# A new order of steps, k filled up to five chunks of 128 rows, and another order of three products, in linear attention followed by a gated FFN

## The chip, the core and the metric

The kernel runs on one core of one Trainium2 chip. The time is that of the core, in microseconds (us), from runs of the same program; less is better. TensorE is called PE here, VectorE DVE, ScalarE ACT and GpSimd POOL; SyncE (SP) issues the DMAs.

## What is computed

```python
# q, k, v: batch 8, heads 8, sequence 576, head size 64
q_s = exp(q - max(q, -1));      q_s = q_s / (sum(q_s, -1) + 1e-9)
k_s = exp(k - max(k, axis=2));  k_s = k_s / (sum(k_s, axis=2) + 1e-9)      # over the sequence
kv  = einsum('bhsd,bhse->bhde', k_s, v)
x   = einsum('bhsd,bhde->bhse', q_s, kv)          # then 4608 tokens x 512
xn  = x / sqrt(mean(x*x, -1) + 1e-6) * rms_g
out = (silu(xn @ w_gate) * (xn @ w_val)) @ w_out  # 512 -> 1536 -> 512
```

## The kernel before

The 4608 tokens lie in nine blocks of 512 (j = 0 to 8), the 1536 inner features in twelve tiles of 128, the eight heads in four pairs (g = 0 to 3). The batches of the attention (b = 0 to 7) are 576 rows long, so blocks and batches overlap unevenly. The FFN is done in three ways. Block 0 works on the weights as they come, in the steps `f1` (L1230, gate and value) and `f2` (L1301, output). Block 1 uses `f1p` (L1246) on f16 pairs of a high and a low word: 24 products of 512 columns for each of its 12 tiles. Its results leave PSUM by `silu1` (L1252, on ACT) and `h_mul1` (L1257, on DVE), and they leave two buffers, the pool `ps_gv`, for the tiles to come. Blocks 2 to 8 use a scheme of seven products, `pp` (L1166), with evictions `ev` and the output product `fu` (L1214).

The weights arrive packed and are unpacked by chains of small steps on ACT and DVE (`conv_*`, lines 437 to 464), cut in words (`w_hi`, `w_lo`), and made into f16 operands for the later blocks (`w_sc`: L388 on ACT over 1024 columns; `b_hi`, `b_lo`, `t_op`, `t_hi`, `t_lo`: casts at L383, sums at L1118, L1126 to L1144). All that has to be there before `pp` can start.

Of the attention, three steps matter here. `k_mm` (L600) forms k's product with v for one batch and head pair: twenty products, ten for each head, the two heads in the two halves of PSUM's partitions. The sequence of 576 rows is taken in four chunks of 128 and one of 64. `q_x` (L796) multiplies the result with q in three products per segment: kv is held as a high and a low word (`hi`, `lo`), q as `qh` and `ql`. `n_sum` (L920) is the sum of squares for the norm: two products with one constant operand.

What every engine does in which order is written out by hand. `ORDER` is a text of 2970 steps. It is read in one pass, and each step appends its instructions to the queues of the engines; a queue is worked off in that order, and an instruction at its head that has to wait holds up all behind it. A step's name is followed by its numbers and, where more than one engine can do it, by the engine: `:A`, `:D` or `:P` for ACT, DVE or POOL.

```python
    with tc.manual_schedule():
        for step in ORDER.split():
            step, _, engine = step.partition(":")
            name, *args = step.split(".")
            unit[0] = where[engine]
            steps[name](*map(int, args))
```

Two kinds of step only keep PE busy: `warm` at the start, and `fill.n`, which adds n products with zeros (L476) to a sum that is open.

Of the kernel before, what the change touches and what calls it, by code (L numbers as in the profile page):

```python
# [29 lines left out]
q_exp.0.0 v_load.0.2 q_max0.0.2 q_sum0.0.0 load_w.0.1 q_sub0.0.1:P fill.2 k_mm.0.0 q_exp.0.3 k_rec.0.2 q_sum0.0.3  # L30
kv_norm0.0.0:A q_sub0.0.2:P load_w.1.1 q_exp.0.1 g_abs q_eps0.0.0 q_exp.0.2 q_rec0.0.0 q_sum0.0.1 v_load.0.1
q_mul0.0.0:P conv_low.0.0.1 kd_load.1.0 k_max.0.1 conv_mul.0.0 fill.12 q_t0.0.0 q_eps0.0.3 k_exp.0.1 conv_shift.0.0
load_w.3.0 k_tr0.2.0 conv_sign.0.0 q_c0.0.0:A k_tr0.2.1 k_ev0.2.0:A q_rec0.0.3 fill.2 q_x0.0.0 load_w.2.2 q_eps0.0.1
q_rec0.0.1 q_mul0.0.3:P k_ev0.2.1:A q_sum0.0.2 load_w.1.2 q_mul0.0.1:P conv_low.3.2.1 k_tr0.3.0 x_hi.0.0:D x_sq.0.0
load_w.2.1 x_lo.0.0 k_tr0.3.1 k_ev0.3.0:A k_mm.0.2 q_eps0.0.2 k_ev0.3.1:A q_load0.1.0 q_rec0.0.2 conv_low.0.1.1
k_eps.0.1 k_rec.0.1 q_mul0.0.2:P conv_mul.0.1 k_mm.0.3 k_load.1.0 conv_low.1.0.2 k_eps.0.3 k_rec.0.3 conv_shift.0.1
k_tr0.1.0 v_load.1.0 kv_norm0.0.3:A k_tr0.1.1 conv_sign.0.1 n_sum0.0 v_load.1.1 kv_norm0.0.2:A k_max.1.0 w_hi.0.0.2:P
q_t0.0.3 conv_mul.1.0 q_t0.0.1 q_c0.0.3:D load_w.4.1 conv_low.3.0.2 conv_shift.1.0 q_x0.0.3 q_c0.0.1:A conv_sign.1.0
w_lo.0.0:P f1.0.0.0.0 x_sq.0.3 f1.0.1.0.0 x_hi.0.3:D s_tr k_ev0.1.0:A kd_load.1.1 x_lo.0.3 w_lo.0.1:P k_ev0.1.1:A
fill.3 k_mm.0.1 conv_low.2.2.1 s_top load_w.0.2 conv_low.1.2.1 s_rows s_bits kv_norm0.0.1:A load_w.4.0 k_rows.1.0  # L40
conv_low.2.0.2 q_x0.0.1 k_load.1.1 q_max0.1.0 q_t0.0.2 x_sq.0.1 x_hi.0.1:D q_load0.1.1 q_sub0.1.0:P q_c0.0.2:A
n_sum0.1 x_lo.0.1 q_load0.1.2 v_ones.1.0 q_exp.1.0 q_x0.0.2 k_sub.1.0 k_load.1.2 v_ones.1.1 f1.0.1.0.1 q_sum0.1.0
conv_mul.1.1 f1.0.1.0.3 f1.0.0.0.1 load_w.5.0 f1.0.0.0.3 x_hi.0.2:D x_sq.0.2 k_exp.1.0 conv_shift.1.1 fill.1 n_sum0.2
conv_sign.1.1 f1.0.1.0.2 f1.0.0.0.2 conv_low.0.2.1 f1.0.0.1.0 x_lo.0.2 f1.0.1.1.0 w_hi.1.0.2:P load_w.5.1 f1.0.1.1.1
# [5 lines left out]
q_sub0.1.1:P g_mul.0 conv_shift.1.2 f1.2.0 w_lo.2.1:P silu.0 conv_sign.1.2 conv_low.6.0.2 v_ones.1.2 h_mul.0  # L50
load_w.5.2 conv_mul.3.0 q_eps0.1.0 g_mul.1 f1.2.1 conv_shift.3.0 silu.1 conv_sign.3.0 g_mul.2 conv_mul.3.1 load_w.7.0
q_max0.1.2 conv_one.3.1 silu.2 conv_shift.3.1 q_sub0.1.2:P conv_low.5.2.1 q_rec0.1.0 k_rows.1.1 k_eps.1.0 k_rec.1.0
conv_sign.3.1:P h_mul.2 kv_norm0.1.0:A h_mul.1 conv_mul.3.2 w_hi.3.0.2:P load_w.7.1 k_max.1.3 f2.0 conv_shift.3.2
kd_load.2.0 q_exp.1.2 conv_sign.3.2 q_exp.1.1 w_lo.3.0:P k_sub.1.1 load_w.7.2 conv_mul.2.2 q_sum0.1.1 conv_mul.4.0
# [20 lines left out]
w_lo.8.1:P q_exp.1.3 g_mul.7 fill.5 n_col.0.0 k_exp.1.2 n_max.0.0 w_lo.7.1:P f1.7.1 conv_sign.11.2 n_sq.0.2 q_sum0.1.3
v_ones.1.3 h_lo.5:P n_sq.1.0 n_col.0.1 w_hi.9.0.2:A h_lo.6:P k_mm.1.2 n_max.0.1 k_rows.1.3 n_sq.1.1 k_eps.1.2
v_load.2.0 f1.8.0 k_rec.1.2 w_lo.9.1:P k_sub.1.3 k_load.2.1 kv_norm0.1.2:A k_exp.1.3 n_bits.0.1.0 q_eps0.1.3
q_rec0.1.3 w_lo.9.0:P k_mm.1.3 g_mul.8 q_mul0.1.3:P silu.7 q_t0.1.1 k_eps.1.3 k_rec.1.3 f1.8.1 silu.8 q_c0.1.1:D
kv_norm0.1.3:A h_mul.7 n_bits.0.1.1 n_bits.0.1.2 n_bits.0.1.5 w_sc.0.1 n_bits.0.1.3 n_bits.0.1.4 q_x0.1.1 h_mul.8
# [1303 lines left out]
```

## Time and profile before

| | |
|---|---|
| median of 3 runs | 934.89 us (933.1, 934.89, 935.95) |
| span of the profiled execution, first to last instruction | 930.9 us |
| median less this span | 4.0 us |
| PE busy | 913.8 us, 98% of the span |
| DVE busy | 617.3 us, 66% |
| ACT busy | 559.1 us, 60% |
| POOL busy | 305.9 us, 33% |

The span is that of one execution under the profiler. The profile lists no other time for it, so the 4.0 us between it and the median are taken as what lies around the span. A busy share is a mean over stages that differ, and PE's share holds the zero products of `fill` and `warm` too.

### The profile page before, as it was taken

The numbers are of one execution on the slowest core, as the hardware profiler recorded it, in microseconds if no ns is written. First come the engines' busy times: TensorE is split into PE (matmuls) and PEld (weight loads), VectorE is DVE, ScalarE is ACT, GpSimd is POOL, SyncE is SP. The second block draws the span as 40 slices with busy tenths as digits, with TensorE's granted clock in tenths as the row PEclk, the third lists the DMA queues.
The fourth block names the chain that finished last, engine by engine and source line by source line (L and its number), as shares of the span: only waits on it lengthen the run. The fifth ranks groups of instructions, "written<-read, shape, count | busy, mean of one in ns | idle before, by whom it ended". The sixth has DMA issues, their size and how long they took to land.

```text
span 930.9 us, 16383 instructions
## 1 busy us (share of the span) xinstructions
PE 913.8 (98%) x6479; PEld 644.0 (69%) x6479; DVE 617.3 (66%) x1330; ACT 559.1 (60%) x880; POOL 305.9 (33%) x304
## 2 busy tenths in 40 slices
...
DMA packets 29550, 68.06 MB, mean 73 GB/s; under 512 B 3744, under 2 KB 4000, under 8 KB 29472
## 3 DMA queue, kind: packets, MB, share of 16 engines
...
## 4 chain that ended last, share of the span: by engine, by line
PE 83%; DVE 6%; ACT 4%; DMA 3%; issue 2%; POOL 1%; SPq 0%; ACTq 0%; POOLq 0%; DVEq 0%
PE ps_gv L1166 38%; PE ps_o L1214 22%; PE ps_o L1301 5%; PE ps_gv L1230 5%; PE ps_gv L1246 4%; PE ps_a L796 2%; PE ps_a L600 2%; DMA qt<-in_q_dram 1%; PE ps_a L560 1%; DMA w_gv<-in_kt_dram 1%; DMA w_br<-in_w_dram 1%; PE ps_a L1021 1%; ACT w_gv L388 0%; PE ps_a L725 0%; DVE x_raw L827 0%
## 5 line engine op out<-in xcount | busy, mean ns | idle before, releaser
L1166 PEld LDWEIGHTS <-w_gv 128*128 128x128 f16 x2016 | 196.0, 98 | 39.7 <-issue 3.2
L1166 PE MATMUL ps_gv<-xo,w_gv 128*128 128x256 f16 x1296 | 155.8, 273 | 0.6 <-ACT w_br L383 0.4
L1166 PE MATMUL ps_gv<-x_op,w_gv 128*128 128x256 f16 x720 | 86.5, 273 | 0.2
L1166 PEld LDWEIGHTS <-w_br 128*128 128x128 f16 x756 | 73.7, 98 | 14.3 <-issue 1.3
L1214 PEld LDWEIGHTS <-hh 128*128 128x128 f16 x504 | 48.9, 98 | 49.8 <-issue 0.4
L1214 PEld LDWEIGHTS <-hl 128*128 128x128 f16 x504 | 49.0, 98 | 47.5 <-issue 0.6
L1214 PE MATMUL ps_o<-w_o,hl 128*128 128x512 f16 x336 | 79.9, 379 | 0.0
L1214 PE MATMUL ps_o<-w_o,hh 128*128 128x512 f16 x336 | 78.4, 379 | 0.0
L1230 PE MATMUL ps_gv<-xo,wf 128*128 128x512 f32 x264 | 66.7, 404 | 0.0
L1166 PE MATMUL ps_gv<-xo,w_br 128*128 128x256 f16 x540 | 66.1, 273 | 0.0
L1230 PEld LDWEIGHTS ps_gv<-xo,wf 128*128 128x128 f32 x264 | 49.0, 188 | 12.9 <-issue 2.8
L1166 PEld LDWEIGHTS <-wf 128*128 128x128 f16 x504 | 49.2, 98 | 8.1 <-issue 0.3
L1181 DVE TENSOR_TENSOR tm<-ps_gv,tm 128x512 f32<-128x512 f32 x29 | 20.0, 689 | 50.9 <-PE ps_gv L1166 47.7
L785 POOL TENSOR_TENSOR ql<-qT,qh 128x512 fp32r<-128x512 f32 x14 | 18.2, 1301 | 87.1 <-ACT qh L383 87.1
L383 ACT COPY ps_gv<-ps_gv 128x512 f32<-128x512 f32 x42 | 24.0, 572 | 36.3 <-PE ps_gv L1166 13.8
L1181 DVE TENSOR_TENSOR w_br<-ps_gv,w_br 128x512 f32<-128x512 f32 x29 | 20.0, 690 | 37.4 <-PE ps_gv L1166 36.8
L1166 PE MATMUL ps_gv<-xo,wf 128*128 128x256 f16 x360 | 43.9, 273 | 0.0
L897 POOL TENSOR_TENSOR acc<-acc,sq 128x512 f32<-128x512 f32 x11 | 14.0, 1270 | 71.8 <-ACT sq L893 71.8
L1246 PE MATMUL ps_gv<-x_op,w_br 128*128 128x512 f16 x144 | 31.9, 379 | 0.0
L383 ACT COPY w_br<-ps_gv 128x512 f32<-128x512 f32 x29 | 17.0, 585 | 23.5 <-PE ps_gv L1166 23.4
L970 POOL TENSOR_TENSOR wf<-w_gv,wf 128x512 fp32r<-128x512 f32 x22 | 28.1, 1293 | 6.7 <-ACT wf L383 6.3
L383 ACT COPY tm<-ps_gv 128x512 f32<-128x512 f32 x29 | 17.0, 585 | 21.5 <-PE ps_gv L1166 21.3
...
## 6 DMA issues: line engine op xcount, KB each, us to landing
...
```

The costliest lines, as they stand in the source:

```text
L383: (e.copy if e is nc.scalar else e.tensor_copy)(dst, src)
L600: nc.tensor.matmul(ps[h * D:(h + 1) * D, :n1], lhsT=ke[:n, h, j], rhs=vt_[b, g][:n, j, h], start=(j == 0), stop=(j == len(rows) - 1))
L785: on(nc.gpsimd).tensor_tensor(out=ql, in0=qT_[j, g], in1=qh_[j, g][0].bitcast(F32), op=ALU.subtract)
L796: nc.tensor.matmul(px[:, c0:c1], lhsT=wt, rhs=mv[:, c0:c1], start=(i == 0), stop=(i == 2))
L897: on(nc.gpsimd).tensor_tensor(out=acc_[j], in0=acc_[j], in1=sq_[j, g], op=ALU.add)
L970: on(nc.gpsimd).tensor_tensor(out=cut(wl[:, a]), in0=W(s, a), in1=cut(wh[:, a].bitcast(F32)), op=ALU.subtract)
L1166: nc.tensor.matmul(pair(ps, i), lhsT=a[:, wt], rhs=y if i else y.rearrange("p (a c) -> p a c", a=2), start=(first and k == 0 and i == 0 an ...
L1181: nc.vector.tensor_tensor(out=v, in0=bank[j, u, 5 if n == 5 else 3], in1=v, op=ALU.add)
L1214: nc.tensor.matmul(po[2 * n + t], lhsT=a[:, o:o + P], rhs=w, start=(u == 0 and i == 0 and p == 0), stop=(u == NU - 1 and i == 1 and p == 2))
L1230: nc.tensor.matmul(pd[s], lhsT=m[:, a, c * P:(c + 1) * P], rhs=X[j, c][x], start=(n == 1), stop=(n == 3 * NKT))
L1246: nc.tensor.matmul(pd[s], lhsT=w[:, wt], rhs=x, start=(c == 0 and p == 0), stop=(c == NKT - 1 and p == 2))
L1301: nc.tensor.matmul(po[t], lhsT=a[:, t * P:(t + 1) * P], rhs=w, start=(i == 0 and n == 0), stop=(i == NF - 1 and n == len(terms) - 1))
```

## The change

`ORDER` is replaced as a whole (2967 steps instead of 2970); it moves almost all steps and gives some another engine. Only two of its lines stand here, the one with the longest `fill` of before and one of after with a shorter `fill` ahead of a `k_mm`. The steps of PE are the same ones, but for the zero products: 53 before, 32 after. The chunks of `k_mm` are all 128 rows long for the batches 1 to 7; the rows past the end of k are -1e30 in DRAM, so that their exponentials are zero (the DMAs have the same sizes as before, since k came padded to five chunks already, with repeated rows). Batch 0 keeps its chunk of 64. In `q_x` the product (hi, ql) comes second and (lo, qh) third. The keys of `po` are bookkeeping: two blocks may now have output sums open at once.

```diff
@@ ORDER
-o_lo.4:P silu.3 conv_sign.5.2 load_w.10.0 conv_mul.5.1 q_max0.1.3 load_w.10.2 fill.20 q_t0.1.0 conv_one.5.1 w_lo.4.1:P
+conv_low.4.0.2 k_max.1.2 load_w.5.2 fill.4 k_mm.1.0 conv_shift.3.0 kd_load.1.3 w_lo.2.0:P f1.2.0 k_eps.1.0
@@ k_mm
-        rows = [min(P, S - c * P) for c in range(C0)]
+        rows = [P if b else min(P, S - c * P) for c in range(C0)]
@@ q_x
-            for i, (wt, mv) in enumerate(((hi, qh), (lo, qh), (hi, ql))):
+            for i, (wt, mv) in enumerate(((hi, qh), (hi, ql), (lo, qh))):
@@ fu (f2 and store likewise)
-                po[t] = ps_o.tile([P, DM], F32, name="ps_o")
+                po[j, t] = ps_o.tile([P, DM], F32, name="ps_o")
@@ layout
+    past = (np.arange(128)[:, None] + 128 * np.arange(5) >= s)[..., None]
-        "k": pairs(k)[1:, :, :, chunks].transpose(0, 1, 3, 2, 4, 5).reshape(b - 1, g, 128, -1),
+        "k": np.where(past, np.float32(-1e30), pairs(k)[1:, :, :, chunks]).transpose(0, 1, 3, 2, 4, 5).reshape(b - 1, g, 128, -1),
```

After's line numbers are one lower than before's in the parts shown below.

**PE, where block 0 turns from `f1` to `f2`.** L1301 is the output product, L1230 a tile's gate or value, L560 a broadcast of k's maxima, L476 a product with zeros; 20 pairs like the last two rows follow each other, then come four products of L712 (a transpose of q). Before:

```order
L560 MATMUL ps_a<-ident,kx 128x128
L1301 MATMUL ps_o<-w_o,tm 128x512 x4
L1230 MATMUL ps_gv<-xo,wf 128x512 x12
L1301 MATMUL ps_o<-w_o,tm 128x512 x4
L476 LDWEIGHTS zero_b
L476 MATMUL ps_o<-ones_b,zero_b 128x512
```

After, the same stretch of PE's queue, from the first L1301 on:

```order
L1300 MATMUL ps_o<-w_o,tm 128x512 x4
L559 MATMUL ps_a<-ident,kx 128x128
L1229 MATMUL ps_gv<-xo,wf 128x512 x12
L1300 MATMUL ps_o<-w_o,tm 128x512 x4
L1229 MATMUL ps_gv<-xo,wf 128x512 x12
L711 MATMUL ps_a<-ident,x_op_94 128x128 x4
L1300 MATMUL ps_o<-w_o,tm 128x512 x4
L1229 MATMUL ps_gv<-xo,wf 128x512 x12
L469 MATMUL ps_gv<-mean_w 128x512 x2
L1229 MATMUL ps_gv<-xo,wf 128x512 x24
```

The twenty zero products are gone from this place and no others stand in for them, but for the two of a `warm`; the products of the next tiles follow at once.

**ACT, around the first `silu1` (L1252; after: L1251), at the start of block 1.** L388 over 1024 columns scales weights for the later blocks, the casts to `w_br` make their high words. Before:

```order
L383 CAST kv<-ot 128x128
L388 ACTIVATE w_gv<-w_gv,sc 128x1024 x2
L383 CAST w_br<-w_gv 128x512
L388 ACTIVATE w_gv<-w_gv,sc 128x1024
L383 CAST w_br<-w_gv 128x512
L388 ACTIVATE w_gv<-w_gv,sc 128x1024
L383 CAST w_br<-w_gv 128x512
L1252 ACTIVATE tm<-ps_gv,ig 128x512
```

After:

```order
L382 CAST kv<-ot 128x128
L382 CAST hh<-tm 128x512
L1251 ACTIVATE tm<-ps_gv,ig 128x512
L387 ACTIVATE w_gv<-w_gv,sc 128x1024 x4
L1251 ACTIVATE tm<-ps_gv,ig 128x512
```

The scales that stood ahead of the first `silu1` now stand behind it.

**DVE, from the first `h_mul1` (L1257; after: L1256) on.** Between it and the second, before has one small instruction:

```order
L1118 TENSOR_TENSOR w_br<-w_gv,w_br 128x512
L1061 TENSOR_SCALAR mx<-mx 128x6
L1044 TENSOR_SCALAR inv<-mx 128x6
L1257 SCALAR_TENSOR_TENSOR tm<-ps_gv,cu,tm 128x512
L1047 TENSOR_SCALAR ig<-inv 128x6
L1257 SCALAR_TENSOR_TENSOR tm<-ps_gv,cu,tm 128x512
```

After has sixteen, the first eleven of which are shown here behind the first `h_mul1`; a copy of 128x128, three small ones and one more L1117 of 128x512 follow, and then the second `h_mul1`:

```order
L1256 SCALAR_TENSOR_TENSOR tm<-ps_gv,cu,tm 128x512
L1117 TENSOR_TENSOR w_br<-w_gv,w_br 128x512
L382 CAST kv<-ot 128x128
L755 TENSOR_REDUCE sm<-qt 128x16
L1048 TENSOR_SCALAR cu<-sc 128x2
L1284 TENSOR_TENSOR hl<-tm,hh 128x512
L1055 TENSOR_SCALAR mx<-ps_a 128x6
L1057 TENSOR_SCALAR mx<-mx 128x6
L1060 TENSOR_SCALAR mx<-mx 128x6
L1063 SCALAR_TENSOR_TENSOR os<-ig 128x6
L1066 TENSOR_TENSOR mx<-mx,os 128x6
L1129 TENSOR_TENSOR w_gv<-w_gv 128x512
```

From the first `h_mul1` to the twelfth and last, DVE's queue holds 49 instructions of 128x512 before and 60 after, and 12 of 64x64 before and 20 after: steps of `t_op`, `kv_hi`, `x_sum` and `q_sub` have come to it from POOL and ACT. Over the whole program ACT has 723 rows instead of 803, POOL 384 instead of 281, DVE 1098 instead of 1115.

## Rows read from the trace of the kernel before

**Rows 1.** The page, part 1: busy us (share of the span) and instructions.

```profile
PE 913.8 (98%) x6479; PEld 644.0 (69%) x6479; DVE 617.3 (66%) x1330; ACT 559.1 (60%) x880; POOL 305.9 (33%) x304
```

**Rows 2.** The page, part 4: the chain that ended last, by engine.

```profile
PE 83%; DVE 6%; ACT 4%; DMA 3%; issue 2%; POOL 1%; SPq 0%; ACTq 0%; POOLq 0%; DVEq 0%
```

**Rows 3.** Windows: length, busy PE, PEld, DVE, ACT, POOL; PE's clock, DMA share, GB/s.

```profile
0.00:40.00 40.00, 34.39 (x206) 22.63 (x207) 27.95 (x62) 27.98 (x54) 18.66 (x37) 1.00 0.97 366
40.00:80.00 40.00, 38.58 (x168) 25.48 (x167) 35.08 (x72) 33.80 (x52) 24.93 (x24) 1.00 0.71 246
80.00:160.00 80.00, 80.00 (x420) 61.88 (x420) 61.37 (x136) 65.48 (x97) 49.24 (x47) 1.00 0.26 85
160.00:270.00 110.00, 106.24 (x605) 54.05 (x604) 79.85 (x184) 83.53 (x133) 69.83 (x65) 1.00 0.23 75
270.00:800.00 530.00, 527.96 (x4153) 388.69 (x4153) 361.40 (x799) 304.00 (x476) 133.94 (x127) 1.00 0.16 50
800.00:931.00 131.00, 126.67 (x936) 91.25 (x933) 51.62 (x83) 44.34 (x73) 9.25 (x7) 1.00 0.05 17
```

**Rows 4.** PE's timeline over one k_mm, in narrow windows: start, us, products under way.

```profile
676.04 0.95 PE L600 MATMUL ps_a<-vt,kt 128*64 128x65 f32 x20
676.15 0.41 PE L600 MATMUL ps_a<-vt,kt 128*64 128x65 f32 x8
676.50 0.43 PE L600 MATMUL ps_a<-vt,kt 128*64 128x65 f32 x4
676.76 0.23 PE L600 MATMUL ps_a<-vt,kt 64*64 64x65 f32 x2
676.92 0.39 PE L1214 MATMUL ps_o<-w_o,hh 128*128 128x512 f16 x1
```

**Rows 5.** PE's groups by line: the products of k_mm for batches 1 to 7.

```profile
L600 PE MATMUL ps_a<-vt,kt 128*64 128x65 f32 (+1 forms) x560 | 26.6, 231 | 1.1 <-ACT kt L573 0.6 <-POOL hh L383 0.6
```

**Rows 6.** PE's timeline at one q_x, and at one n_sum.

```profile
745.47 0.71 PE L796 MATMUL ps_a<-qh,kv 128*128 128x512 f32 x2
746.02 0.40 PE L796 MATMUL ps_a<-ql,kv 128*128 128x512 f32 x1
...
689.92 0.47 PE L920 MATMUL ps_a<-qh,mean_w 128*128 128x512 f32 x1
690.47 0.39 PE L1166 MATMUL ps_gv<-x_op,w_br 128*128 128x256 f16 x2
```

**Rows 7.** PE's timeline at the longest fill.

```profile
65.43 4.51 PE L476 MATMUL ps_o<-ones_b,zero_b 128*128 128x512 bf16 x20
69.79 0.60 PE L712 MATMUL ps_a<-ident,x_op 128*128 128x128 f32 x4
```

**Rows 8.** PE's timeline at its two longest waits after 160 us (wait and releaser in brackets).

```profile
168.62 0.59 PE L1246 MATMUL ps_gv<-x_op,w_bx 128*128 128x512 f16 x2 [1.45 <-ACT tm L1252]
...
270.18 1.47 PE L1166 MATMUL ps_gv<-xo,w_bx 128*128 128x256 f16 x12 [1.65 <-ACT ps_gv L383]
```

**Rows 9.** ACT's timeline at the first silu1.

```profile
167.89 0.68 ACT L1252 ACTIVATE tm<-ps_gv,ig 128x512 f32<-128x512 f32 x1
```

**Rows 10.** DVE's timeline among the first tiles of block 1.

```profile
163.19 0.28 DVE L645 TENSOR_TENSOR kv<-ot,kv 128x128 fp32r<-128x128 f32 x1
169.83 0.69 DVE L1144 TENSOR_TENSOR w_gv<-w_gv 128x512 f16<-128x512 f32 x1
171.19 1.65 DVE L1118 TENSOR_TENSOR w_br<-w_gv,w_br 128x512 f16<-128x512 f32 x1
172.91 0.74 DVE L1257 SCALAR_TENSOR_TENSOR tm<-ps_gv,cu,tm 128x512 f32<-128x512 f32 x1
176.86 0.75 DVE L1257 SCALAR_TENSOR_TENSOR tm<-ps_gv,cu,tm 128x512 f32<-128x512 f32 x1 [2.30 <-PE ps_gv L1246]
```

**Rows 11.** POOL's timeline at the same moment.

```profile
170.72 1.57 POOL L1118 TENSOR_TENSOR w_br<-w_gv,w_br 128x512 f16<-128x512 f32 x1 [4.19 <-ACT w_br L383]
```

**Rows 12.** Window from the first h_mul1 to the last, columns as in rows 3.

```profile
172.90:268.70 95.80, 94.79 (x548) 47.74 (x547) 69.38 (x162) 69.95 (x112) 64.36 (x60) 1.00 0.26 83
```

More of the change, by code (lines that the diff above doesn't have):

```diff
@@ L30 @@
[L30 to L44, printed above, removed]
@@ L50 @@
[L50 to L54, printed above, removed]
@@ L75 @@
[L75 to L79, printed above, removed]
@@ L120 @@
-q_load.3.2 kv_lo.3.0 h_hi.19:A q_lo.2.3:D v_ones.3.2 t_hi.1.1:A q_max2.3.0 h_lo.19:P q_x.2.3 q_max.3.2 f1p.20.1
-silu1.20 q_sub.3.0:P x_raw.2.3:D x_sq.2.3 t_lo.1.1:D x_acc.2.3:D t_hi.1.2:A f1p.21.0 o2_lo.9 n_hi.2:A h_mul1.20
-t_lo.1.2:P h_hi.20:A n_lo.2:D t_hi.1.3:A n_sum.2 h_lo.20:D silu1.21 f1p.21.1 n_t.2 t_lo.1.3:P n_y0.2 n_y1.2 t_op.4.0:P
-q_exp.3.0 t_hi.2.0:A f1p.22.0 t_op.4.1:P n_rows.2 q_sum.3.0 x_nrm.2.3:P q_half2.3.0 f2.19 silu1.22 h_mul1.21
-x_nrm.2.1:P q_half.3.1 h_hi.21:A x_nrm.2.2:P f2.20 x_nrm.2.0:D q_sum2.3.0 o_x_hi.2.0:A q_rec.3.0 x_sum.2.1:P
@@ new lines @@
+load_w.0.0 kd_load.0.2 warm.2.5 g_load k_max.0.3 warm.2.4 v_load.0.0 k_max.0.0 k_exp.0.3 warm.2.0 q_load0.0.1 warm.2.6
+k_exp.0.0 k_eps.0.3 load_w.0.1 k_tr0.3.1 k_tr0.3.0 warm.2.2 v_load.0.2 q_max0.0.0 k_ev0.3.0:A k_tr0.0.1 k_tr0.0.0
+q_max0.0.3 q_sub0.0.0:P v_load.0.3 warm.2.8 k_eps.0.0 k_rec.0.0 k_rec.0.3 warm.2.11 k_ev0.0.0:D kv_zero0.1 q_exp.0.0
+kv_zero.2 load_w.3.1 k_ev0.0.1:A q_sum0.0.0 conv_low.0.0.1 q_sub0.0.3:P k_max.0.1 kd_load.1.0 load_w.3.0 q_exp.0.3
+k_ev0.3.1:D q_eps0.0.0 q_rec0.0.0 k_max.0.2 v_load.0.1 fill.10 k_mm.0.0 q_mul0.0.0:P k_exp.0.2 load_w.1.1 warm.2.9
@@ new lines @@
+kv_norm0.0.0:D q_sum0.0.3 warm.2.3 conv_mul.0.0 q_max0.0.1 k_exp.0.1 q_load0.1.0 q_eps0.0.3 q_sub0.0.1:P fill.3
+k_tr0.1.0 q_rec0.0.3 q_max0.0.2 q_t0.0.0 load_w.1.0 q_sub0.0.2:D k_tr0.2.1 warm.2.12 q_mul0.0.3:P q_exp.0.1 k_load.1.0
+exp_table g_abs q_c0.0.0:D conv_low.0.1.1 conv_shift.0.0 q_exp.0.2 kv_zero.0 fill.4 q_t0.0.3 conv_sign.0.0 load_w.1.2
+warm.2.1 q_c0.0.3:A q_sum0.0.1 k_mm.0.3 k_ev0.2.1:A load_w.0.2 conv_mul.0.1 q_eps0.0.1 k_tr0.2.0 q_sum0.0.2
+kv_norm0.0.3:A q_eps0.0.2 q_rec0.0.1 q_x0.0.0 load_w.3.2 k_ev0.2.0:D conv_low.3.0.2 q_mul0.0.1:P q_rec0.0.2 k_mm.0.2
@@ new lines @@
+conv_shift.0.1 k_ev0.1.0:A q_mul0.0.2:P q_load0.1.1 x_hi.0.0:D k_tr0.1.1 q_t0.0.1 k_ev0.1.1:A warm.2.10 x_lo.0.0
+load_w.2.0 q_c0.0.1:A k_mm.0.1 x_sq.0.0 conv_sign.0.1 k_load.1.2 k_eps.0.1 q_x0.0.3 w_hi.0.0.2:P k_rec.0.1 k_eps.0.2
+k_rec.0.2 kv_norm0.0.2:D kv_norm0.0.1:D q_t0.0.2 load_w.2.1 conv_low.1.0.2 x_hi.0.3:D w_lo.0.1:P q_x0.0.1 x_lo.0.3
+v_load.1.1 x_sq.0.3 f1.0.0.0.0 kv_zero.1 x_hi.0.1:D q_c0.0.2:A x_sq.0.1 fill.2 q_x0.0.2 x_lo.0.1 load_w.2.2 q_max0.1.0
+f1.0.1.0.0 x_sq.0.2 f1.0.1.0.1 k_max.1.0 q_sub0.1.0:P conv_low.0.2.1 kd_load.1.1 conv_mul.1.0 n_sum0.0 n_sum0.1
@@ new lines @@
+conv_sign.3.0 k_rec.1.0 w_lo.2.1:P q_max0.1.2 conv_mul.3.1 load_w.7.0 v_load.1.2 conv_one.3.1 q_eps0.1.0 k_load.2.2
+h_mul.0 q_sub0.1.2:P conv_low.4.2.1 conv_shift.3.1 f1.2.1 g_mul.2 conv_sign.3.1:P conv_low.6.0.2 q_sum0.1.1
+kv_norm0.1.0:D silu.2 q_rec0.1.0 q_eps0.1.1 h_mul.1 q_mul0.1.0:P conv_mul.3.2 f2.0 conv_mul.2.2 conv_shift.3.2
+w_hi.3.0.2:P q_load.2.0 conv_low.5.2.1 conv_shift.2.2 load_w.7.1 v_ones.1.1 k_max.1.3 w_lo.3.1:P conv_sign.3.2
+q_exp.1.2 conv_sign.2.2 load_w.7.2 conv_mul.4.0 q_rec0.1.1 q_sum0.1.2 k_rows.1.1 q_mul0.1.1:P conv_one.4.0
@@ new lines @@
+q_c0.1.1:D w_sc.0.1 b_hi.0.0:P k_mm.1.3 g_mul.9 w_lo.10.0:P n_col.1.0 b_hi.0.3:A n_bits.0.1.4 k_load.2.1 f1.9.1
+q_max2.2.1 b_hi.0.1:P n_max.1.0 b_lo.0.3:D b_lo.0.1:P k_eps.1.3 k_rec.1.3 b_lo.0.0:D kv_norm0.1.3:A q_x0.1.1
+w_hi.11.0.2:P t_op.0.0:D silu.9 n_col.1.1 f2.5 x_sq.1.1 w_lo.11.1:D t_hi.0.0:P x_raw.1.1:A h_mul.9 b_hi.0.2:A
+x_acc.1.1:D n_sq.2.0 h_hi.7:P n_max.1.1 b_lo.0.2:D f2.6 o_hi.7:A t_op.0.1:D n_sq.2.1 o_lo.7:P h_mul.8 h_hi.8:A
+t_lo.0.0:P n_col.2.1 o_hi.8:A q_t0.1.2 h_lo.8:P n_max.2.1 n_sq.3.1 t_op.0.2:D n_col.2.0 f1.10.0 n_sq.3.0 w_lo.11.0:P
@@ new lines @@
+b_hi.4.2:P o_bits.4 t_op.2.2:D b_lo.3.2:P w_sc.5.1 f1p.13.1 kv_lo.1.1 b_hi.4.3:A t_op.1.0:P o_bits.5 b_hi.4.1:A
+o_bits.6 o_bits.7 b_hi.3.0:A b_hi.5.3:A b_lo.4.1:D b_lo.4.3:P f1p.14.0 h_mul1.13 b_lo.3.0:D h_hi.13:A h_lo.13:P
+store.0.0:D f1p.14.1 t_op.3.0:D silu1.14 b_hi.5.2:A o2_hi.3 b_lo.5.2:P o2_hi.2 o2_lo.3 o2_hi.1 f1p.15.0 o2_hi.0
+o2_lo.2 h_hi.12:A h_mul1.14 t_hi.1.0:A o2_lo.1 b_hi.3.1:A h_lo.12:D f1p.15.1 store.0.2:A b_lo.4.2:D kv_hi.1.3:A
+silu1.15 o2_lo.0 h_hi.14:A b_lo.3.1:D o2_hi.5 h_lo.14:P q_max.2.2 f1p.16.0 b_hi.4.0:A h_mul1.15 b_lo.5.1:P q_half2.2.1
@@ new lines @@
+o2_lo.5 b_lo.5.0:P f1p.16.1 t_op.2.3:D silu1.16 store.0.1:A h_hi.15:P o2_hi.4 t_op.3.1:D k_load.2.3 o2_hi.7 v_ones.2.3
+t_lo.1.0:P f1p.17.0 k_eps.2.0 h_mul1.16 h_lo.15:D b_lo.3.3:P k_rec.2.0 k_max.3.0 kd_load.3.1 f1p.17.1 t_op.3.2:P
+silu1.17 o2_hi.6 t_op.1.1:P o2_lo.6 f1p.18.0 q_half.2.2 o2_hi.10 h_mul1.17 q_sum2.2.1 o2_lo.7 q_rec.2.1 f1p.19.0
+k_sub.2.1 silu1.18 q_mul.2.1:P q_half.2.3 b_lo.5.3:P t_op.1.2:D k_exp.2.1 f1p.18.1 o2_hi.9 o2_lo.4 store.0.3:A
+t_hi.1.1:A o2_hi.8 t_lo.1.1:D k_seg.2 o2_lo.8 q_max2.2.2 k_load.3.1 q_max2.2.3 q_sub.2.2:D f2.12 q_sub.2.3:P q_exp.2.2
@@ new lines @@
+q_sum.2.2 t_hi.1.2:P k_max.3.1 t_lo.1.2:P f2.13 h_mul1.18 kd_load.3.2 h_hi.16:A v_load.2.2 t_op.1.3:P q_t.2.1
+q_exp.2.3 o2_hi.11 k_sub.2.2 q_load.3.0 o2_lo.9 k_exp.2.2 f1p.19.1 o_bits.8 kv_hi.2.0:D t_hi.1.3:A q_sum.2.3 h_hi.17:A
+t_lo.1.3:P kv_lo.2.0 b_lo.4.0:D h_lo.16:D f2.14 t_op.4.0:P k_eps.2.1 silu1.19 k_rec.2.1 kv_hi.2.1:D q_max.3.0
+v_ones.2.2 t_hi.2.0:P q_half.3.0 t_op.3.3:P kv_lo.1.2 q_x.2.0 f2.15 x_sq.2.0 q_half2.2.2 x_raw.2.0:A q_max2.3.0
+q_sub.3.0:D q_hi.2.1:A kv_lo.2.1 h_hi.18:A q_lo.2.1:P q_half2.2.3 k_seg.3 q_sum2.2.3 q_sum2.2.2 h_lo.17:P q_rec.2.2
@@ new lines @@
+v_load.3.1 f2.16 k_max.3.2 q_mul.2.2:P o2_lo.10 kd_load.3.3 k_load.3.0 t_op.4.1:P k_sub.2.3 f2.17 q_rec.2.3 k_exp.2.3
+k_eps.2.2 k_rec.2.2 t_op.4.2:P kv_hi.2.2:D q_exp.3.0 h_lo.18:D t_op.4.3:P kv_lo.2.2 k_seg.4 q_t.2.2 v_load.3.0
+h_mul1.19 v_ones.3.1 f2.18 q_mul.2.3:P k_load.3.2 kv_lo.1.3 h_hi.19:A q_load.3.1 t_lo.2.0:P k_eps.2.3 k_sub.3.0
+k_max.3.3 k_exp.3.0 h_lo.19:P q_x.2.1 kd_load.4.0 v_ones.3.0 f2.19 q_hi.2.2:A x_raw.2.1:A q_lo.2.2:P x_sq.2.1
+t_hi.2.1:A x_acc.2.1:D t_lo.2.1:P q_t.2.3 q_x.2.2 k_rec.2.3 q_sum.3.0 q_load.3.3 t_op.5.0:P f1p.20.0 x_sq.2.2
@@ new lines @@
+kv_hi.2.3:D kv_lo.2.3 x_raw.2.2:A q_hi.2.3:A q_lo.2.3:D q_half2.3.0 q_x.2.3 q_sum2.3.0 q_rec.3.0 x_acc.2.2:D k_seg.5
+x_sq.2.3 f1p.20.1 k_eps.3.0 q_mul.3.0:D x_acc.2.3:P k_max.4.0 q_t.3.0 kd_load.4.1 silu1.20 n_hi.2:P v_load.3.3
+x_raw.2.3:A q_load.3.2 f1p.21.0 n_lo.2:P h_mul1.20 k_load.3.3 q_max.3.1 h_hi.20:P q_half.3.1 h_lo.20:P k_rec.3.0
+kv_hi.3.0:D n_sum.2 kv_lo.3.0 silu1.21 q_hi.3.0:P f1p.21.1 k_sub.3.1 n_t.2 k_exp.3.1 n_y0.2 n_y1.2 t_hi.2.2:A k_seg.6
+t_lo.2.2:P k_load.4.0 f1p.22.0 v_load.3.2 n_rows.2 x_nrm.2.3:D x_nrm.2.1:P h_mul1.21 q_max2.3.1 f2.20 x_nrm.2.2:P
```

483 lines of the change are left out of this document (231 added, 252 removed).

## The prediction

> **What bounds the kernel now.** I read the page's busy times first: PE is busy 913.8 of 930.9 us and no other engine reaches 70% [rows 1]. The chain that ended last says the same: 83% of it is PE's own work [rows 2]. So time comes from two places only: work that PE does, and gaps or filler in its queue. The windows say where those gaps are [rows 3]. The granted clock is 1.00 in every stage, the upper of the two levels, so there is nothing to win or lose there at first sight. PE's idle time is window less busy: 5.6 us up to 40, 1.4 from 40 to 80, none from 80 to 160, 3.8 from 160 to 270, 2.0 from 270 to 800, and 4.3 behind 800, most of it the last eviction and store, which no order of steps removes. Up to 40 us the DMA engines are busy 0.97 of the time, so data come as fast as they come. From 40 to 80 us DVE (35.08 of 40) and ACT (33.80) are nearly full as well: weights are being unpacked, and PE's 38.58 there hide filler. From 270 us on PE runs alone: what is to be had there is PE's own work.
>
> The sum is made against the profiled execution's span, 930.9 us. The median of the runs is 934.89, so 4.0 us lie around the span, and I add them at the end.
>
> **k_mm.** The form in the rows changes from 128*64 to 64*64 for the last chunk [rows 4]. The twenty products go in ten pairs, the two heads of a chunk side by side. The first pair starts at 676.04, the second at 676.15 and the eighth, the last with 128 rows, at 676.50: six steps of 0.058 us. The tenth starts at 676.76, and the next work of PE at 676.92. From the eighth pair to that next work it is 0.42 us. With one form for all ten pairs I put 0.06 for eighth to ninth, 0.06 for ninth to tenth, and leave the way out at 0.16: 0.28, so 0.14 less. There are 560/20 = 28 such steps for batches 1 to 7 [rows 5], all on PE, which bounds: 28 x 0.14 = **3.9 us less**. The bounds: nothing, if a pair of 128 rows behind another one costs as much as the two odd intervals (the steady 0.058 speaks against it); and 28 x 0.24 = 6.7, if the way out falls to 0.06 too (the way in, 0.11 against 0.058, says that a change of form costs something anyhow). I take 3.9. The subtraction and the exponential of k already run over five full chunks and the DMAs keep their sizes, so no other engine pays.
>
> **q_x.** The same products with the same operands in another order. Could the second product with `hi` be cheaper because its operand stands there already? `n_sum` has just that, two products with one constant operand, and takes 690.47 - 689.92 = 0.55 us for two; the first two of `q_x`, which have two different ones, take 746.02 - 745.47 = 0.55 [rows 6]. So **0**; the bounds are those two-digit rows' rounding, 0.01 for each of some 50 segments, 0.5 us either way. `ql` is now needed one product (0.24 us) earlier and `lo` as much later, which is little beside the steps between.
>
> **The order up to 160 us.** PE executes 53 - 32 = 21 zero products fewer. One takes (69.79 - 65.43)/20 = 0.218 us [rows 7], so they are worth 21 x 0.218 = 4.6 us if useful work comes as early as the fill ends, and nothing if PE then waits for the weights instead. Twenty stood at 65.43, where the new queue goes on with the next tiles. DVE and ACT are 88% and 85% busy there [rows 3], so weights can arrive a little sooner, not much: their free 4.9 and 6.2 us in that stage are about what would have to be gained. The order also puts three `kv_norm0`, two `k_ev0` and one `q_sub0` on DVE ahead of the third tile; at 0.69 for a 128x512 [rows 10] that is at most 4.1 us on the engine that is fullest, though ACT is relieved by as much. I take half of the fills: **2.3 us less**. Bounds: the 4.6, and 1.4 of idle time from 40 to 80 on top; on the other side 4.1 - 2.3, some 2 us more.
>
> **The order from 160 us on.** The two longest waits are 1.45 and 1.65 us [rows 8]. The first: PE wants a buffer that the first `silu1` has to empty, and ACT gets to it only at 167.89 [rows 9], behind four scales and three casts in its queue (the order shows them). In the new queue the scales and these casts stand behind it, so this wait should go. The second: `pp` waits for a copy on ACT between its first two products, with one `f2` between them; in the new order an `f2` and a third product of twelve matmuls lie between, some 1.3 us more of cover (the row's twelve take that). Together 3.1 us. Against it stands DVE's queue. Between the first and second `h_mul1` DVE had 3.95 us, 2.30 of it idle [rows 10]; now it has four instructions of 128x512 and a reduction there, at 0.69, and eleven of 128x128 and less, at 0.28 or below: at most 6.5 us. That is up to 2.6 more than the old distance, and `h_mul1` frees a buffer of PE. From the first to the last `h_mul1` DVE is busy 69.38 of 95.80 us [rows 12]; 11 more instructions of 0.69 and 8 small ones of at most 0.28 make 79.2, 83%. It still fits, but a queue at 83% is late now and then. I take half of the 3.1: **1.5 us less**. Bounds: the whole 3.8 + 2.0 of idle time; on the other side the rival with DVE below.
>
> A rule that bears on this stage: the Trainium skill, page "SBUF — State Buffer", section "SBUF: two separate sides", says that a DVE instruction with two inputs in SBUF and a POOL instruction that reads SBUF exclude each other for a whole instruction. The trace agrees: the L1118 of 1.65 us on DVE stands beside one of 1.57 on POOL, where a like one took 0.69, and L1257, which reads PSUM, keeps to 0.74 and 0.75 [rows 10, 11]. By that rule the eleven added instructions are exposed; as an estimate, POOL runs 64.36/95.80 = 67% of this stage and half of 1.57 is lost at each meeting: 11 x 0.67 x 0.79 = 5.8 us more on DVE, 85 of 95.8, and the sum stays as it is.
>
> **The sum:** 3.9 + 0 + 2.3 + 1.5 = 7.7 us less, a span of 923.2 and with the 4.0 around it **927.2 us**. About 0.3% (2.8 us) is what a measurement of this kernel can tell from no change: below 932.1 is faster, above 937.7 slower.
>
> **The rivals.**
> *The order gives nothing.* PE waits where it filled, because DVE and ACT set the pace from 40 to 80 us [rows 3]; other small waits replace those two. Only k_mm is left: 934.9 - 3.9 = 931.0, with some us either way, so partly within the 0.3%. For it: nearly full engines. Against it: 13% and 15% of slack in them.
> *The order gives all.* The fills' 4.6 and the idle 1.4 + 3.8 + 2.0 go as well: 3.9 + 4.6 + 7.2 = 15.7, 919.2 us. Against it: some of these waits are the start of a product on a result just made, and remain in any order.
> *k_mm does not do what it says:* the odd intervals are those of the end of a sum and not of the 64-row form. Then 2.3 + 1.5 remain, 931.1. Against it: the intervals grow exactly where the form changes.
> *Slower: DVE becomes the bound in block 1.* With 79.2 us of work in 95.8, seventeen more instructions that take 1.65 instead of 0.69 [rows 10] fill it ((95.8 - 79.2)/0.96 = 17). POOL has gone from 281 to 384 rows, so such meetings will be more frequent, and every late `h_mul1` holds a buffer of PE. From 17 on each costs 0.96 us; the 6.2 of the other terms and 2.8 more are used up at 27. At half of the sixty, 30, it is 79.2 + 28.8 - 95.8 = 12.2: 934.9 - 6.2 + 12.2 = 940.9. Against it: the trace shows such long instructions as exceptions, and ACT has become freer.
>
> **Chances.** The sum as made, 922 to 932: 0.53. Order gives nothing: 0.15, three fifths of it below 932.1. Order gives all: 0.13. No gain from k_mm: 0.07, half of it below 932.1. DVE the bound: 0.12, a quarter of it within 0.3%. So faster: 0.52 + 0.09 + 0.13 + 0.035, about 0.77; same 0.14; slower 0.09. For the range I leave out the lower half of "all" and the upper two thirds of "DVE the bound": 920 to 936.5.
>
> **What would show it.** In the changed profile one k_mm should take 0.74 us from its first start to the next work, with no 64*64 form. The two intervals of q_x's first products should stay 0.55 together. Zero products: 32, none near 65 us; if PE's idle time from 40 to 80 rises from 1.4 towards 6, they became waits. The wait for L1252's successor should be gone, and that of `pp` for ACT's copy below 0.5. DVE between the first and last h_mul1 should be about 79 to 85 us busy; if PE waits there for DVE by more than 2 us in all, or the stage from 160 to 270 grows, the slower rival has come. Wrong I would be, above all, by the early stage: its order is new from the first step on, and a weight that comes 3 us later there is seen by every step behind it.

## The result: 923.4 us against 934.0, and the profile after

The changed kernel takes 923.4 us (median of 4 runs, 922.16 to 923.96) against 934.0 (4 runs, 932.7 to 935.95): a ratio of 0.9886, 95% interval 0.9869 to 0.9902, so 9 to 12 us less. The forecast was 927.2, in a range of 920 to 936.5.

The profiled execution took 923.09 us by the clock of the runs and 921.3 by its span, so 1.8 us lie around the span, as in every run of the experiments below. If before's execution is read the same way it took 930.9 + 1.8 = 932.7, and one of its runs has just that time. The 4.0 us that the prediction added were thus too many by 2.2. By spans the change is worth 930.9 - 921.3 = 9.6 us.

The page's busy times after, as in [rows 1]:

```profile
PE 906.7 (98%) x6458; PEld 639.0 (69%) x6458; DVE 618.6 (67%) x1330; ACT 511.5 (56%) x779; POOL 406.9 (44%) x409
```

PE has 21 instructions fewer, the zero products. ACT has 101 instructions and 48 us fewer, POOL 105 instructions and 101 us more, about twice the time for each. Next the windows up to 270 us, with the columns of [rows 3].

```profile
0.00:40.00 40.00, 36.09 (x212) 22.40 (x212) 29.13 (x76) 24.00 (x43) 16.06 (x32) 1.00 0.92 345
40.00:80.00 40.00, 38.13 (x160) 25.72 (x161) 37.79 (x76) 34.89 (x51) 30.76 (x32) 1.00 0.80 280
80.00:160.00 80.00, 77.62 (x403) 58.71 (x402) 70.68 (x131) 67.82 (x100) 58.95 (x57) 1.00 0.25 83
160.00:270.00 110.00, 109.79 (x656) 57.28 (x654) 97.48 (x214) 68.16 (x103) 73.94 (x69) 1.00 0.23 74
```

Against [rows 3] the idle time of PE has changed places: from 160 to 270 us it went from 3.8 to 0.2, from 80 to 160 it rose from none to 2.4 (from 40 to 80, where the twenty zero products went, only from 1.4 to 1.9). From 80 us on DVE is now fuller than ACT; from 160 to 270 it is busy 97.48 of 110 us where it had 79.85, and ACT is down from 83.53 to 68.16.

The two long waits of [rows 8] are gone. From 160 to 300 us the list of PE's waits (in all, times, longest) has only this line:

```profile
PE ps_a L599 <- PE ps_o L1300: 0.2, 1, 0.2
```

One `k_mm` after, in the narrow windows of [rows 4]:

```profile
659.80 0.34 PE L599 MATMUL ps_a<-vt,kt 128*64 128x65 f32 x4
660.38 0.23 PE L599 MATMUL ps_a<-vt,kt 128*64 128x65 f32 x2
660.54 0.28 PE L1165 MATMUL ps_gv<-xo,w_br 128*128 128x256 f16 x1
```

From its first start to PE's next work it is 660.54 - 659.80 = 0.74 us; in [rows 4] it was 0.88. The tenth pair begins at 660.38, 0.58 behind the first, where it was 0.72. The way out stayed at 0.16. The whole group is down from 26.6 to 22.5 us busy ([rows 5]).

```profile
L599 PE MATMUL ps_a<-vt,kt 128*64 128x65 f32 x560 | 22.5, 227 | 0.5 <-issue 0.3 <-PE ps_o L1300 0.2
```

### The profile page after: what moved, and what is told of

It reads as the page before. It is cut to its first block, busy times and chain, and to the rows that moved or that the text cites. A ratio compares the mean times of both kernels' runs of the same rounds, so it can differ in the third digit from the quotient of the medians.

```text
span 921.3 us, 16357 instructions
## 1 busy us (share of the span) xinstructions
PE 906.7 (98%) x6458; PEld 639.0 (69%) x6458; DVE 618.6 (67%) x1330; ACT 511.5 (56%) x779; POOL 406.9 (44%) x409
## 4 chain that ended last, share of the span: by engine, by line
PE 90%; DVE 6%; issue 2%; POOL 1%; ACT 1%; DMA 1%; DVEq 0%; POOLq 0%; ACTq 0%; SPq 0%
PE ps_gv L1165 41%; PE ps_o L1213 23%; PE ps_gv L1245 7%; PE ps_o L1300 7%; PE ps_gv L1229 4%; PE ps_a L795 2%; PE ps_a L599 2%; PE ps_a L559 1%; PE ps_gv L469 1%; DVE ps_a L455 1%; PE ps_a L1020 0%; PE ps_a L919 0%; DMA w_br<-in_w_dram 0%; DVE w_gv L463 0%; DMA qt<-in_q_dram 0%
## 5 line engine op out<-in xcount | busy, mean ns | idle before, releaser
L826 POOL TENSOR_TENSOR x_raw<-x_raw,acc 128x512 f32<-128x512 f32 x17 | 24.4, 1455 | 23.7 <-DVE acc L946 19.1
L1201 POOL TENSOR_TENSOR hh<-w_br,hh 128x512 f16<-128x512 f32 x7 | 8.1, 1157 | 57.7 <-ACT hh L382 57.7
L896 POOL TENSOR_TENSOR acc<-acc,sq 128x512 f32<-128x512 f32 x14 | 18.3, 1310 | 31.7 <-ACT sq L892 31.7
```

Of the source, the lines that this page charges most:

```text
L826: on(nc.vector).tensor_tensor(out=XR[:, g], in0=XR[:, g], in1=r_[j], op=ALU.mult)
L896: on(nc.gpsimd).tensor_tensor(out=acc_[j], in0=acc_[j], in1=sq_[j, g], op=ALU.add)
```

## The experiments

All kernels compute the whole function; where zero products are left out, they are products that add nothing. Before, run beside them on the same chips, had medians of 933.6 to 934.3 us.

**1. The full chunks alone, in the old order.**

```diff
-        rows = [min(P, S - c * P) for c in range(C0)]
+        rows = [P if b else min(P, S - c * P) for c in range(C0)]
```

(and k's rows past the end at -1e30, as in the change)

> The order of before with the full chunks alone. Theory (each change of form costs 0.10 to 0.16 us beside a steady 0.058): a k_mm takes 0.73 us instead of 0.88, 28 x 0.147 = 4.1 us less, 929.9 us against 934.0, all of it on PE and from the second batch on. Rival (the saving is taken up by the next wait, since the order was made for the longer k_mm): 932 to 934. Rival (the product itself was cheap, and the change's gain is that of the order): 934.

Measured: 930.32 us against 934.33, ratio 0.9966 (0.9954 to 0.9979), by the medians 4.0 less, by the interval 2.0 to 4.3. The theory stands within that: a `k_mm` takes 0.74 us in this trace. From the first `pp` to the end the kernel needs 663.95 us, and before needs 930.9 - 264.47 = 666.43: 2.5 less for the 18 steps there, 0.14 for each, so nothing waited in their place. For the ten steps ahead the two traces show no gain (the first `pp` starts at 264.35 and 264.47 us).

**2. The changed kernel with the short chunk put back.** The same line, the other way round.

> The changed kernel with the short last chunk put back. Theory: 923.4 + 4.1 = 927.5 us, k_mm at 0.88 us again. Rival (in the new order other waits cover a part of it): 924 to 926.

Measured: 926.33 us, ratio to before 0.9912 (0.99 to 0.9925), against 0.9886 for the change: 2.9 more by the medians, 2.4 by the ratios. That lies between the theory's 4.1 and the rival's upper end of 2.6. In the new order the step is worth a little less than in the old one, or the same within what the runs can tell.

**3. The changed kernel with q_x's products in the old order.**

```diff
-            for i, (wt, mv) in enumerate(((hi, qh), (hi, ql), (lo, qh))):
+            for i, (wt, mv) in enumerate(((hi, qh), (lo, qh), (hi, ql))):
```

> The changed kernel with q_x's products in the old order. Theory: no difference, 923.4 within 0.5 us, since two products with one operand took the same 0.55 us as two with different ones. Rival (ql, which comes from a subtraction on POOL or DVE, is now awaited one product earlier, so that the old order is better): 922 to 923, with waits for ql gone from L796. Rival (an operand that stands there already is cheaper): 925 to 927.

Measured: 923.1 us (922.96 to 923.76), ratio 0.9881 (0.9868 to 0.9894). No difference, as the theory had it.

**4. The old order without its longest fill.** `fill.20` is taken out of ORDER, nothing else.

> The order of before without the twenty zero products at 65 us. Theory (weights set the pace there, PE only waits where it filled): within 1 us of before, 933 to 934, with some 4 us of new idle time of PE behind 65 us. Rival (the fill is work that PE does in place of useful work): 4.4 us less, 929.6. Rival (without it PE's clock falls for a time): slower than before, with a granted clock below 1.00 in the slices behind 65 us.

Measured: 934.84 us against 934.33, ratio 1.0009 (0.9999 to 1.0019). The timeline of PE at the place shows what came instead of the twenty products of [rows 7], and the windows give the clock (the eighth figure, behind the busy times):

```profile
71.23 0.97 PE L712 MATMUL ps_a<-ident,x_op 128*128 128x128 f32 x4 [4.28 <-DVE w_o L464]
```

```profile
71.23:72.20 0.97, 0.97 (x5) 0.97 (x6) 0.57 (x2) 0.94 (x3) 0.97 (x2) 0.57 1.06 321
72.00:73.00 1.00, 1.00 (x3) 0.48 (x3) 0.93 (x2) 0.73 (x2) 1.00 (x2) 0.50 0.88 266
75.00:77.00 2.00, 2.00 (x6) 0.95 (x5) 0.77 (x2) 2.00 (x4) 0.40 (x1) 1.00 0.87 320
72.00:80.00 8.00, 8.00 (x23) 4.68 (x23) 6.17 (x10) 6.55 (x12) 5.37 (x6) 0.83 0.59 217
```

Twenty products of 0.218 are 4.36 us, and 4.28 of them became a wait for DVE, which unpacks weights. So the fill cost nothing where it stood. Behind the gap the granted clock is 0.50, the lower of the two levels (1.2 GHz), until shortly before 75 us and 1.00 again from there; the four transposes take 0.97 us instead of 0.60 [rows 7]. The last window's 0.83 is the mean of both. Theory and the rival of the clock are both right in part: no gain, and a fall of the clock, but a loss of 0.5 us by the medians that the interval does not tell from none.

**5. The new order up to block 1 only.** The new ORDER to its first `f1p`, then all steps that are left in the old order; full chunks.

```diff
@@ ORDER, at the seam (behind the last step ahead of f1p.12.0.0 in the new order)
+q_max.2.2 n_sq.3.2 n_max.4.0 n_sq.4.2 o_x_lo.1.0:D n_col.4.1 n_max.4.1 n_sq.5.1 n_bits.1.3.5 n_col.5.0 n_max.5.0 n_sq.5.2
+n_col.5.1 f1p.12.0.0 n_max.5.1 kv_hi.1.0:A n_bits.3.6.0 o_x_lo.1.2:D n_fro f1p.12.0.1 kv_lo.1.0 ...
```

> The changed kernel, with the new order up to the first product of block 1 (161 us in before) and from there on the steps that are left in the order of before. With the old order throughout and full chunks it was 930.3 us, with the new order throughout 923.4. Theory (most of the order's 6.9 us come from block 1 and later, since up to block 1 waits took the fills' place): 928.5 to 930. Rival (the zero products that went are the gain): 925 to 926. The seam, where some steps of the first part are made up in one go, may cost up to 1 us.

Measured: 931.7 us, ratio 0.9976 (0.9967 to 0.9986), above both. The waits of PE around the seam and windows behind it:

```profile
PE ps_a L1021 <- ACT kv L1014: 2.2, 1, 2.2
PE ps_a L1021 <- DVE mx L1029: 1.1, 2, 0.9
```

```profile
164.13:166.00 1.87, 1.87 (x7) 0.96 (x6) 1.47 (x5) 0.48 (x3) 0.00 (x0) 0.50 0.00 0
166.00:168.00 2.00, 2.00 (x8) 0.83 (x7) 0.76 (x2) 0.00 (x0) 0.00 (x0) 0.50 0.00 0
170.00:172.00 2.00, 2.00 (x10) 0.94 (x10) 0.37 (x1) 1.59 (x3) 0.00 (x0) 1.00 0.00 0
```

The seam itself cost 3.3 us of waits, for the steps made up in one go, and behind them some 5 us at the lower clock, 0.50 up to 168 us and 1.00 from 170. That is more than the 1 us that the expectation allowed for, so this run says nothing sure on the order ahead of it.

**6. The new order up to block 2.** Made in the same way with the seam at the first `pp`, where only eight steps had to be made up.

> The same with the seam at the first product of block 2 (264 us in before). Theory (block 1 gives some 3.5 us, by the two long waits that are gone and the smaller ones; the blocks behind it 1 to 2): 924.5 to 926. Rival (the blocks from 2 on hold the gain, since most of PE's time lies there): 928 to 930.

Measured: 926.0 us, ratio 0.9916 (0.9904 to 0.9929). The windows from the first `pp` to the end, of experiment 1, of this one and of the changed kernel in turn (length, then PE's busy time with its number of products):

```profile
264.35:928.30 663.95, 656.31 (x5111) 481.06 (x5109) 418.21 (x886) 350.30 (x552) 145.34 (x136) 1.00 0.14 43
```

```profile
264.25:924.50 660.25, 652.84 (x5078) 479.08 (x5075) 410.16 (x876) 345.88 (x546) 139.74 (x133) 1.00 0.13 44
```

```profile
263.71:921.30 657.59, 651.40 (x5078) 479.37 (x5075) 389.42 (x844) 319.16 (x488) 230.91 (x227) 1.00 0.13 44
```

The first two run the old order behind the first `pp`, which they reach at the same time, 264.3 us; but the second has 33 products fewer still to do. The new order had done these by then, and that is 663.95 - 660.25 = 3.7 us. The second and the third have the same 5078 products left, and the third needs 660.25 - 657.59 = 2.7 us less for them: that is the new order of the later blocks, with POOL at 227 instructions where it had 133, and ACT and DVE at fewer. So the gain of the order has two parts, some 3.7 us up to block 2 and 2.7 behind it; by the medians they are 930.32 - 926.0 = 4.3 and 926.0 - 923.4 = 2.6. The stretch behind the first `pp` is 657.59 to 657.66 us in all five traces with the new order there (the change, experiments 3, 8, 9 and 10), but 665.2 to 666.4 in four with the old one (before, experiments 4, 7 and 11), so each part is known to about 1 us. The time is at the upper end of the theory's range, with more behind block 2 than the theory had; the rival's 928 to 930 did not come.

**7. The two long waits taken out by hand, in the old order.**

```diff
@@ ORDER, block 1 (what lies between is left as it is)
-w_sc.1.1 ... b_hi.1.2:A ... w_sc.2.0 f1p.12.0.2 ... silu1.12 ... fill.2 f1p.13.0 ... h_mul1.12
+f1p.12.0.2 silu1.12 w_sc.1.1 b_hi.1.2:A ... w_sc.2.0 ... f1p.13.0 h_mul1.12
@@ ORDER, block 2
-pp.2.0.2 ... pp.2.0.6
+pp.2.0.6 pp.2.0.2 ...
```

> The order of before, with three moves: the first silu1 ahead of two scales and a cast on ACT (and the two zero products behind it left out), the first h_mul1 ahead on DVE, and block 2's third product (a form that needs no new buffer) ahead of its second. Theory (the two long waits are made by the order alone): 1.45 and 0.4 us less in the first place, 1.3 less in the second, 931.2 against 934.3. Rival (the wait moves to the next buffer or to the next operand, because the scales come later): 933.5 to 934.5, with the same idle time of PE between 160 and 180 us.

Measured: 934.95 us against 933.62, ratio 1.0011 (1.0001 to 1.0021). PE's waits from 160 to 300 us:

```profile
PE ps_gv L1166 <- ACT ps_gv L383: 1.5, 1, 1.5
PE ps_o L1301 <- ACT hh L383: 1.3, 1, 1.3
PE ps_o L1301 <- DVE hl L1285: 1.2, 1, 1.2
```

The rival was right. The wait for `silu1` is gone, but the next product of PE, L1301, now waits for its operands: `hh`, which stood behind the same scales on ACT, and `hl`, which stood on DVE behind the moved `h_mul1` and sums of weights that had themselves waited for ACT's casts. That is 1.3 + 1.2 us instead of 1.45 and two zero products, and PE is idle for 2.55 us between 160 and 180 where before has 1.45. And in front of `pp` the third product, put ahead, waits for ACT's copy just as the second did: 1.5 us here, 1.65 in [rows 8]. Here the wait that one sees was the first of a row of late results.

**8. The changed kernel without its 32 zero products.** All `fill` steps are taken out of ORDER.

> The changed kernel without its 32 zero products. Theory (like the twenty at 65 us, they stand where PE would wait): 923 to 925, idle time in their place, and where they are missing for long a granted clock below 1.00 for some us behind. Rival (they are work in the way): 32 x 0.218 = 7 us less, 916.4.

Measured: 921.63 us (921.05 to 922.22), ratio 0.9872 (0.9859 to 0.9884), by the medians 1.8 less than with them, though the intervals of the two ratios overlap. The window up to the first gate product:

```profile
0.00:26.00 26.00, 20.96 (x158) 15.37 (x158) 18.79 (x48) 15.62 (x30) 12.71 (x29) 1.00 0.94 347
```

The clock is 1.00, though PE is idle for 5.0 of these 26 us. Over the whole span PE is busy 7.1 us less and idle 5.7 us more (20.3 where it was 14.6), so most of the 7 us became waits, as the theory had it. The first gate product starts at 25.81 us here and at 27.16 in the changed kernel, 1.35 us sooner, and the lead lasts to the end. But that this is the zero products' doing is not shown: in five more traces that run the changed kernel's order up to there (experiments 2, 3, 5, 6 and 10) it starts anywhere from 26.62 to 27.76. By the medians this is the fastest of all the kernels.

**9. Without the first 25 of them only.**

> The changed kernel without the first 25 zero products (all before 46 us), with the other 7. Without all 32 it was 921.6 against 923.4. Theory (the first 17 are in the way: without them the first gate product began 1.35 us sooner, and the lead stays to the end): 921.6 to 922. Rival (the later 7, at 50 and 154 us, cost the difference): 923.4.

Measured: 921.97 us (921.74 to 922.89), ratio 0.9873 (0.986 to 0.9887). By the medians the gain of experiment 8 comes from these. But in this kernel's trace, which has the order of experiment 8 up to the first gate product, that product starts at 26.87 us, 1.06 later than there, and the span is 921.1 us, 0.2 under that of the change. So the 1.35 us, on which this experiment's theory rested, are hardly more than what two executions differ by. Whether leaving the zero products out gains 0.2 or 1.4 us, and where, is not settled.

**10. More work on DVE in block 1.** In the changed kernel, 14 steps between the first `f1p` and the first `pp`.

```diff
-b_lo.3.2:P ... t_lo.1.0:P ...
+b_lo.3.2:D ... t_lo.1.0:D ...
```

> The changed kernel with 14 more subtractions (b_lo, t_lo) on DVE instead of POOL between the first product of block 1 and the first of block 2. DVE is busy 92.5 of 104.8 us there; 14 x 0.69 = 9.7 more make 102.2, 98% of the stage. Theory (DVE has room up to the length of the stage, but a queue that full is late for h_mul1 and PE then waits): 2 to 6 us slower than the changed kernel, 925.5 to 929.5, with waits of PE for DVE's tm. Rival (POOL and DVE get in each other's way less with less on POOL, so DVE's mean instruction is shorter): 923 to 924.5. The rival of the prediction (each costs its 0.96 from the seventeenth on): no change at 14.

Measured: 930.05 us, ratio 0.9961 (0.9948 to 0.9973), 6.7 us more than the change. PE's waits from 158 to 275 us, and windows behind the first:

```profile
PE ps_a L599 <- DVE kv_lo L650: 3.9, 1, 3.9
PE ps_a L795 <- DVE ql L784: 1.2, 1, 1.2
```

```profile
220.00:224.00 4.00, 2.93 (x25) 2.18 (x26) 2.64 (x12) 0.00 (x0) 1.92 (x2) 0.53 0.14 36
224.00:228.00 4.00, 4.00 (x14) 1.47 (x12) 3.79 (x9) 1.26 (x2) 3.84 (x5) 0.62 0.60 209
228.00:232.00 4.00, 4.00 (x37) 2.20 (x36) 3.29 (x8) 0.62 (x1) 1.97 (x2) 1.00 0.00 0
```

Fourteen subtractions of 0.69 us, 9.7 in all, are less than the 12 us that DVE had free, and yet 6.7 came through to the time, a little above the theory's 2 to 6. PE did not wait for `h_mul1`, which both the prediction and this expectation watched. It waited 3.9 us in `k_mm`, which writes into a PSUM buffer of the pool that `kv_lo` (two subtractions of 64x64 on DVE) had still to read, and 1.2 us in `q_x` for its operand `ql`. Behind the longer wait the clock was low for some 7 us. By the profiles' busy times 4.3 us of the loss are idle time of PE and 2.7 longer busy time.

**11. The old order without all its 53 zero products.**

> The order of before without its 53 zero products. Without the twenty at 65 us alone it was 934.8 against 934.3. Theory (they stand where PE waits, and their absence costs clock where the gap is long): 933 to 936, with a granted clock below 1.00 behind the longest gaps. Rival (the first ones are in the way here too): 932 or less.

Measured: 934.47 us against 933.64, ratio 1.0007 (0.9996 to 1.0018). The theory holds: the old order gains nothing by leaving them out. From 0 to 40 us the granted clock is 0.91 and from 40 to 65 it is 0.93, where before has 1.00 [rows 3]:

```profile
0.00:40.00 40.00, 32.16 (x180) 21.72 (x181) 26.22 (x59) 26.93 (x53) 16.81 (x35) 0.91 0.96 361
40.00:65.00 25.00, 22.78 (x101) 16.06 (x100) 21.32 (x50) 18.37 (x27) 13.82 (x13) 0.93 0.68 229
```

## Why the forecast was right in direction and too small in size

**k_mm, 3.9 us less: right.** The profile shows 0.14 us for such a step, with the way out unchanged, as assumed, and the whole group's busy time fell by 4.1. Alone it brought 4.0 by the medians, 2.0 to 4.3 by the interval (experiment 1), and 2.9 was lost when it was undone (experiment 2).

**q_x, nothing: right.** 923.1 us with the old order of its products and 923.4 with the new one (experiment 3). That `ql` is awaited one product earlier costs nothing that these runs can tell.

**The order up to 160 us, 2.3 less: the number came, but not from where it was put.** Block 1 begins at 158.91 us instead of 161.26:

```profile
0.00:158.91 158.91, 150.74 (x768) 106.23 (x768) 136.69 (x280) 126.72 (x193) 104.69 (x118) 1.00 0.56 199
158.91:263.71 104.80, 104.59 (x616) 53.43 (x615) 92.49 (x208) 65.63 (x98) 71.29 (x66) 1.00 0.23 73
```

That is 2.35, as forecast, but by luck. Twelve products of L1020 (three `n_col`, 0.44 us for four in a row, so some 1.3) have been moved behind this point, and four of the shorter `k_mm` (0.6), a term of its own, lie ahead of it. What is left is about 0.5 us. The traces do not give it closely: with the same order up to here, experiments 3, 6 and 10 reach block 1 at 158.83, 159.49 and 157.72 us, and experiment 1, with the old order and full chunks, at 161.72, so by the pair that one takes it is 0 to 2.7. Half of the fills' time was no source for it: in the old order nothing is gained without them (experiments 4 and 11). The argument about full engines was the better one (DVE's slack there is 12%, not the 13% that one of the rivals states).

**The order from 160 us on, 1.5 less: the step that was mis-sized.** The prediction took half of the two longest waits and left the rest as a bound. In block 1 PE is busy 104.59 of 104.80 us now: all of its idle time there went, while the products of this stage rose. Counted up to block 2 the order's gain is 3.7 us (experiment 6), of which the traces do not say how much belongs to the stage ahead of 160 us; behind block 2 it is 2.7, where the prediction had nothing, since the windows of [rows 3] show only 2.0 us idle in 530. That was no proof that nothing was to be had: of the 2.7 only 1.2 are idle time (7.4 us before it, 6.2 now), and the busy time itself fell from 652.84 to 651.40 for the same 5078 products. Waits shorter than what is left of the product ahead may hide in it; no row here shows them one by one, and why the busy time fell stays open. So the order gave 3.7 + 2.7 = 6.4 instead of 3.8 by spans, and 6.9 by the medians (930.32 - 923.4).

**The mechanism given for it was wrong in part.** The wait for `silu1` did go, and the copy ahead of `pp` came in time. But experiment 7 shows that moving the steps named is not enough: the waits behind them take over. The new order moved their neighbours as well and gave many steps another engine; which of these moves bring the gain was not separated.

**The rivals.** That the order gives nothing or k_mm nothing is excluded by experiments 1, 2 and 6. The slower rival, DVE as the bound in block 1, did not come, but its point was set much too high: not 17 lengthened instructions, 16 us, could be taken in, but less than 9.7 us of work (experiment 10). From the first `h_mul1` to the last, as in [rows 12], DVE is busy 82.84 us, within the 79 to 85 that the prediction named, 88% of the stage, and the list of PE's waits above has none for DVE:

```profile
166.85:261.08 94.23, 94.02 (x528) 47.33 (x527) 82.84 (x187) 57.96 (x86) 64.11 (x60) 1.00 0.25 80
```

The prediction expected more meetings of DVE and POOL because POOL has more rows in the whole program; in this stage POOL is busy 64.11 us, where it had 64.36. DVE's timeline between the first two `h_mul1` (L1256), against [rows 10]:

```profile
166.85 0.75 DVE L1256 SCALAR_TENSOR_TENSOR tm<-ps_gv,cu,tm 128x512 f32<-128x512 f32 x1 [0.20 <-PE ps_gv L1245]
169.14 1.10 DVE L1284 TENSOR_TENSOR hl<-tm,hh 128x512 fp32r<-128x512 f32 x1
172.41 1.25 DVE L644 TENSOR_TENSOR kv<-ot,kv 128x128 fp32r<-128x128 f32 x1
175.33 0.74 DVE L1256 SCALAR_TENSOR_TENSOR tm<-ps_gv,cu,tm 128x512 f32<-128x512 f32 x1
```

It is 8.5 us from the one to the other, where the prediction had at most 6.5, because some instructions were stretched: 1.25 for a 128x128 that took 0.28 in [rows 10], with an L1117 of 1.67 us on POOL beside it, from 171.84 on. PE is busy all of 160 to 180 us nevertheless.

**The base.** 2.2 us of the miss (927.2 against 923.4) are no term of the change: the span of one execution was set against the median of others, with 4.0 us around it where 1.8 are.
